# A fused recurrence and feed-forward kernel: copies shared with ScalarE, borrowed PSUM banks, a reordering store, unread matmuls and a fourth pair unit

One Trainium2 chip, one core. The metric is device time in microseconds (us) of one execution, median of several; lower is better.

## The reference

A gated linear recurrence for 4 batches of 8 heads, 768 steps, head size 48; its output is the input of a two-layer network with exact GELU.

```python
f = 1 / (1 + exp(-f_logit))
for t in range(768):
    state = f[:, :, t, :, None] * state + outer(k[:, :, t], v[:, :, t])
    y[:, :, t] = q[:, :, t] @ state
x = y.transpose(0, 2, 1, 3).reshape(3072, 384)
h = x @ w_in                       # 384 x 2048
g = 0.5 * h * (1 + erf(h / sqrt(2)))
return g @ w_out                   # 2048 x 384
```

## The kernel before

Sequences are cut into 24 chunks of 128 steps, two chunks to a unit, one feed-forward group for each unit. The kernel lists all operations with a guessed duration each. A greedy scheduler in the kernel's own Python sets the order of each engine, and also which buffer an operation gets. So the order on an engine is fixed before the run, and a wrong guess becomes a wait.

A "pair" unit puts steps 2p and 2p+1 next to each other, which lets its loads move 384-byte runs in place of 192. Then position j*64+p of a chunk's tile is step 2p+j, and something must put the steps back in order. Before, the copy of the transposed output did it:

```python
SIZES = [2] * 12
PAIRS = [0, 1, 2]
LOADS = ["u0", "u1", "i0", "i1", "i2", "i3", "u2", "o0", "o1", "o2", "o3"]   # then u3 ... u11
# ... (cut)
        def xcopy():                                     # xT: input of the first layer
            to = xT.t()[:, :, j * C:(j + 1) * C]
            if pair:
                nc.vector.tensor_copy(to.rearrange("a i (p s) -> a i s p", s=2),
                                      xpv().rearrange("a i (s p) -> a i s p", s=2))
            else:
                nc.vector.tensor_copy(to, xpv())
# ... (cut)
            P.add("DMA", 0.55, lambda n=n, osb=osb: nc.sync.dma_start(
                out=out[n * C:(n + 1) * C, :], in_=osb.t()), ...)      # the store of 128 rows
```

Loads of q, k, v and f_logit and all stores are issued by SP, in the order of its program. Weights are issued by GpSimd. TensorE's results go through eight PSUM banks: four for the feed-forward layers, two for attention's scores, two for the rest.

## Time and profile before

| | kernel before |
|---|---|
| median of 3 runs | 203.27 us (203.03 to 203.34) |
| profiled span | 200.9 us |
| TensorE / ScalarE / VectorE busy | 91% / 71% / 52% |
| DMA, mean over the span | 135 GB/s |

The lines that carry the reading of stages stand in the prediction. Loads and stores come through one queue; an issue takes 0.4 to 2.1 us between 40 and 64 us.

```profile
43.09 0.97 SPq L673 DMA_DIRECT2D out_dram<-osb  x2
44.11 0.45 SPq L351 DMA_DIRECT2D kt<-in_k_dram  x1
44.61 0.70 SPq L351 DMA_DIRECT2D qt<-in_q_dram  x1
45.35 1.00 SPq L351 DMA_DIRECT2D vt<-in_v_dram  x1
```

The first two stores are issued in 0.97 us and the next load follows at once. In the packets of the trace, the first store's 128 rows take 0.74 us from the first start to the last end.

### The profile page before, as it was taken

How to read it: one execution, taken by the hardware profiler on the slowest of the kernel's cores; microseconds unless marked ns; L12 is line 12 of the kernel's file. 1: busy time of each engine (PE TensorE's matmuls, PEld its weight loads, DVE VectorE, ACT ScalarE, POOL GpSimd, SP SyncE). 2: the span in 40 equal slices, each digit the busy share in tenths (PEclk: the TensorE clock that was granted, in tenths of full speed). 3: DMA queues.
4: the chain of work that ended last, by engine and by line, in shares of the span. 5: the costliest groups of instructions: out<-in, count | busy, mean ns of one | idle time of the engine just before them, and what ended most of it. 6: DMA issues, size and time to landing. Idle time of an engine off the chain costs nothing.

```text
span 200.9 us, 4982 instructions
## 1 busy us (share of the span) xinstructions
PE 182.2 (91%) x2010; PEld 141.7 (71%) x2010; DVE 103.7 (52%) x210; ACT 143.4 (71%) x243; POOL 52.4 (26%) x116
## 2 busy tenths in 40 slices
PE   0677989999989997997999999999999999999992
PEld 0446667687678687666868958967877969696961
DVE  4479661274386685887559728759778400000000
ACT  3642069989899979986999999769565828273740
POOL 7369236041133434105145411115303000000000
PEclk9999999999999999999999999999999999999999
DMA  6999999999899989989999993011001011110102
GB/s 155 261 224 172 175 269 189 182 220 202 181 216 195 182 203 186 203 177 210 182 197 214 191 214 96 3 39 39 3 0 65 16 42 39 38 44 11 68 0 78
DMA packets 93013, 27.04 MB, mean 135 GB/s; under 512 B 87872, under 2 KB 92480, under 8 KB 92992
## 3 DMA queue, kind: packets, MB, share of 16 engines
q1 hardware_dynamic: 90816, 23.60, 53.7%
q0 software_dynamic: 2176, 3.15, 9.4%
q8 instruction: 15, 0.25, 0.5%
q14 instruction: 6, 0.05, 0.1%
HBM read 25.17 MB, written 4.72 MB: 149 GB/s over the span
## 4 chain that ended last, share of the span: by engine, by line
PE 57%; ACT 20%; DMA 13%; SPq 3%; issue 3%; DVE 2%; POOL 1%; ACTq 0%; DVEq 0%
PE ps L667 25%; PE ps L652 20%; ACT L692 8%; ACT gT L657 6%; DMA fl<-in_f_logit_dram 5%; DMA win<-in_moe_w_in_dram 4%; DMA kt<-in_k_dram 3%; PE ps L444 3%; SPq L345 2%; ACT fl L368 2%; PE ps L535 2%; ACT lf L373 2%; PE ps L506 1%; ACT rg L400 1%; PE ps L385 1%
## 5 line engine op out<-in xcount | busy, mean ns | idle before, releaser
L652 PE MATMUL ps<-xT,win 128*128 128x256 bf16 x576 | 72.7, 277 | 3.1 <-ACT gT L657 3.0
L667 PE MATMUL ps<-wout,gT 128*128 128x384 bf16 x384 | 70.1, 326 | 0.4 <-DMA wout<-in_moe_w_out_dram 0.2
L652 PEld LDWEIGHTS <-win 128*128 128x128 bf16 x576 | 61.4, 115 | 6.0 <-issue 3.5
L657 ACT ACTIVATE gT<-ps 128x512 bf16<-128x512 f32 x96 | 53.1, 602 | 7.9 <-PE ps L652 5.6
L667 PEld LDWEIGHTS <-gT 128*128 128x128 bf16 x384 | 35.1, 97 | 21.3 <-ACT gT L657 1.3
L692 ACT ACT_TABLE_LOAD x29 | 37.2, 1283 | 0.5
L413 DVE TENSOR_TENSOR kp<-kt,rg 128x384 bf16<-128x384 f32 x24 | 13.9, 579 | 24.1 <-ACT rg L400 24.0
L671 ACT ACTIVATE osb<-ps 128x384 f32<-128x384 f32 x24 | 11.8, 493 | 20.2 <-PE ps L667 20.0
L456 DVE TENSOR_TENSOR am<-ps,mask 128x512 bf16<-128x512 f32 x36 | 23.1, 684 | 5.9 <-PE ps L535 5.8
L419 POOL CAST vb<-vt 128x384 bf16<-128x384 f32 x24 | 13.1, 554 | 43.7 <-DMA vt<-in_v_dram 43.4
L482 POOL TENSOR_TENSOR tn<-rr,gl 128x384 f32<-128x384 f32 x16 | 13.6, 850 | 41.5 <-DVE rr L480 38.7
L368 ACT ACTIVATE fl<-fl 128x768 f32<-128x768 f32 x12 | 10.3, 859 | 18.0 <-DMA fl<-in_f_logit_dram 17.9
L498 DVE CAST yb<-ps 128x384 bf16<-128x384 f32 x24 | 13.0, 553 | 11.9 <-PE ps L557 9.0
L449 DVE COPY kq<-ps 128x1024 bf16<-128x1024 bf16 x24 | 16.4, 685 | 3.3 <-PE ps L444 3.1
L487 POOL CAST sb<-tn 48x192 bf16<-48x192 f32 x40 | 15.3, 383 | 8.4 <-DVE tn L476 6.5
L400 ACT ACTIVATE rg<-ps 128x384 f32<-128x384 f32 x24 | 11.9, 495 | 6.8 <-PE ps L387 3.5
L416 DVE TENSOR_TENSOR qp<-qt,gt 128x384 bf16<-128x384 f32 x24 | 14.4, 601 | 0.2 <-ACT gt L402 0.2
L402 ACT ACTIVATE gt<-ps 128x384 f32<-128x384 f32 x24 | 11.9, 496 | 0.0
L444 PE MATMUL ps<-ident,kp 128*128 128x128 bf16 x96 | 10.2, 234 | 0.3 <-DVE kp L413 0.3
L456 DVE TENSOR_TENSOR am<-ps,maskp 128x512 bf16<-128x512 f32 x12 | 7.7, 685 | 5.4 <-PE ps L583 5.4
L444 PE MATMUL ps<-ident,qp 128*128 128x128 bf16 x96 | 10.2, 234 | 0.3 <-DVE qp L416 0.3
L373 ACT ACTIVATE lf<-fl 128x768 bf16<-128x768 f32 x12 | 10.1, 843 | 0.3
(58 smaller groups left out, 150.6 us busy)
## 6 DMA issues: line engine op xcount, KB each, us to landing
out_dram<-osb SPq DMA_DIRECT2D x24, 192.0 KB, 1.9
fl<-in_f_logit_dram SPq DMA_DIRECT2D x18, 192.0 KB, 3.8
kt<-in_k_dram SPq DMA_DIRECT2D x18, 192.0 KB, 3.7
qt<-in_q_dram SPq DMA_DIRECT2D x18, 192.0 KB, 3.8
vt<-in_v_dram SPq DMA_DIRECT2D x18, 192.0 KB, 3.7
win<-in_moe_w_in_dram POOLq DMA_DIRECT2D x4, 384.0 KB, 8.2
wout<-in_moe_w_out_dram POOLq DMA_DIRECT2D x4, 384.0 KB, 6.7
fl<-in_f_logit_dram SPq DMA_DIRECT2D x3, 384.0 KB, 4.2
```

The source lines that it names most:

```text
L368: P.add("ACT", 0.72, lambda: nc.scalar.activation(fl.t(), fl.t(), AF.Exp, scale=-1.0), rd=[("fl", n) for n in ns], wr=[("e", u)], bufs=[fl ...
L373: nc.scalar.activation(lf.t()[:, :, :, 0:D], v, AF.Ln, bias=1.0)
L400: P.add("ACT", 0.40, lambda g=gps[j], rg=rg: nc.scalar.activation(rg.t(), g.t()[:, 0:HD], AF.Exp, scale=-1.0), rd=[("g", n)], wr=[("rg", n ...
L416: P.add("DVE", 0.475, lambda y=y, gt=gt, j=j: nc.vector.tensor_tensor(y["qp"].t()[:, :, 0:D], half(u, x["qt"], j), gt.t().rearrange("p (h ...
L444: nc.tensor.transpose(tpv()[:, i, p, :], sr.t()[:, 2 * p:2 * p + 2, :], ident)
L449: P.add("DVE", 0.61, lambda tpv=tpv, kqv=kqv: nc.vector.tensor_copy(kqv(), tpv().rearrange("a i p (c t) -> a (i p) c t", c=2) if U[u]["pai ...
L456: P.add("DVE", 0.61, lambda hh=hh: nc.vector.tensor_tensor(ams[hh].t(), aps[hh].t().rearrange("p (h t) -> p h t", t=C), mk.unsqueeze(1).to ...
L487: P.add("POOL", 0.36, lambda hh=hh: nc.gpsimd.tensor_copy(sb.t()[64 * hh:64 * hh + D, :, D * hh:D * hh + D], tn.t()[64 * hh:64 * hh + D, : ...
L652: nc.tensor.matmul(hps.t()[:, i * tok:(i + 1) * tok], col(fo)[:, kk, :], xT.t()[:, kk, :], start=(kk == 0), stop=(kk == KO - 1))
L657: acts.append(P.add("ACT", 0.50, lambda u=u, hps=hps: nc.scalar.activation(gT.t()[:, u * pk:(u + 1) * pk, :].rearrange("p a b -> p (a b)") ...
L667: nc.tensor.matmul(op.t()[:, 0:d_model], gT.t()[:, fo, s_ * C:(s_ + 1) * C], wout[fo // 4][:, fo % 4, :], start=(fo == 0), stop=(fo == FO ...
L692: nc.scalar.preload_act_table_set({"exp": "natural_log_exp_and_others", "gelu": "gelu_and_others"}[o.table])
```

## The change

Its intent is a faster start (a warm TensorE, less on VectorE, no waits for the two attention banks), cheaper xT copies, fewer small load packets, and a scheduler with durations nearer to the trace. A warm TensorE is one at its full clock; unread matmuls, products of zeros whose result nobody reads, are to bring it there early.

```diff
-PAIRS = [0, 1, 2]
+PAIRS = [0, 1, 2, 3]
+EARLY = [0, 1]          # cumulative sums of these units use feed-forward banks
+HELP = [0, 1]           # ScalarE takes v casts, kq, yb and xT copies of these units
+WARM = 30.0             # unread matmuls in gaps that the plan shows before this time
@@ the store puts the steps in order, the copy no longer does
+    def rows(n):
+        r = out[n * C:(n + 1) * C, :]
+        return r.rearrange("(p j) m -> j p m", j=2) if U[n // 2]["pair"] else r
-            nc.vector.tensor_copy(to.rearrange(...), xpv().rearrange(...))    # pair units
+            copier(help_)(xT.t()[:, :, j * C:(j + 1) * C], xpv())
-                nc.sync.dma_start(out=out[n * C:(n + 1) * C, :], in_=osb.t())
+                nc.sync.dma_start(out=rows(n), in_=osb.t())
@@ unit 0's second score block
-            aps = [s_ap.new(), s_ap.new()]
+            aps = [(s_fh if jk and u == 0 else s_ap).new() for _ in range(2)]
@@ unread matmuls into the bank that the next real operation opens
+            if o.opens is not None and o.start < WARM:
+                for _ in range(int((o.start - at - 0.25) / (0.11 if o.start < 10 else 0.06))):
+                    nc.tensor.matmul(o.opens.t()[:, 0:C], junk, junk, start=True, stop=True, ...)
@@ durations in the plan: pair loads 1.2 -> 1.45, w_in 2.2 -> 2.56, w_out 2.2 -> 2.15,
@@ exponentials 0.72 -> 0.84, several matmul groups shorter; and a new rule for changing tables
```

More of the change, by code (lines that the diff above doesn't have):

```diff
@@ L59 @@
     __slots__ = ("eng", "dur", "fn", "bufs", "prio", "deps", "table", "start", "end", "vis", "seq", "name",
-                 "left", "outs", "inst", "chain")
+                 "left", "outs", "inst", "chain", "opens", "lag")
 class Plan:
@@ L68, in __init__, with add @@
         self.ops, self.w, self.r = [], {}, {}
-    def add(self, eng, dur, fn, rd=(), wr=(), bufs=(), prio=0.0, deps=(), table=None, name="", chain=None):
+    def add(self, eng, dur, fn, rd=(), wr=(), bufs=(), prio=0.0, deps=(), table=None, name="", chain=None, opens=None, lag=0.0):
         o = Op()
@@ L73, in add @@
         o.start = o.end = o.vis = o.inst = None
-        o.chain = chain
+        o.chain, o.opens, o.lag = chain, opens, lag
         o.seq = len(self.ops)
@@ L94, in run @@
         free["DMA"] = 1.8
-        act = None
+        act, switched = None, 0.0
         for o in self.ops:
@@ L108, in run @@
                 for d in o.deps:
-                    v = d.end if d.eng == o.eng and (o.eng != "DMA" or d is o.chain) else d.vis
+                    v = d.end if d.eng == o.eng and (o.eng != "DMA" or d is o.chain) else d.vis + o.lag
                     t = v if v > t else t
@@ L123, in run @@
                 if o.table and act and o.table != act:
-                    x = max(t, min(t + 2 * TABLE, max([d.vis for d in o.deps] + [0.0]) + PATIENCE))
+                    x = max(t, min(t + 2 * TABLE, max([d.vis for d in o.deps] + [switched]) + PATIENCE))
                 key = (int(x * 20 + 0.999), o.prio, o.seq)
@@ L132, in run @@
             if o.table and o.table != act:
-                act = o.table
+                act, switched = o.table, t
                 d += TABLE
@@ L158 @@
 SIZES = [2] * 12
-PAIRS = [0, 1, 2]
+PAIRS = [0, 1, 2, 3]
+EARLY = [0, 1]
+HELP = [0, 1]
+XDMA = []
+KDMA = []
+WARM = 30.0
 LOADS = ["u0", "u1", "i0", "i1", "i2", "i3", "u2", "o0", "o1", "o2", "o3"]
@@ L346 @@
                         out=x[nm].t().rearrange("p (h x) -> p h x", h=H), in_=srcp(a, m)),
-                        [(nm, 2 * m), (nm, 2 * m + 1)], [x[nm]], 1.2, f"{nm}{m}")
+                        [(nm, 2 * m), (nm, 2 * m + 1)], [x[nm]], 1.45, f"{nm}{m}")
             else:
@@ L355 @@
             load("pool", lambda m=m: nc.gpsimd.dma_start(out=win[m], in_=win_src[:, :, 512 * m:512 * m + 512]),
-                 [f"win{m}"], [], 2.2, what)
+                 [f"win{m}"], [], 2.56, what)
         else:
-            load("pool", lambda m=m: nc.gpsimd.dma_start(out=wout[m], in_=wo_src[m]), [f"wout{m}"], [], 2.2, what)
+            load("pool", lambda m=m: nc.gpsimd.dma_start(out=wout[m], in_=wo_src[m]), [f"wout{m}"], [], 2.15, what)
     def decays(u):
@@ L367, in decays @@
         flv = fl.t
-        P.add("ACT", 0.72, lambda: nc.scalar.activation(fl.t(), fl.t(), AF.Exp, scale=-1.0),
+        P.add("ACT", 0.84, lambda: nc.scalar.activation(fl.t(), fl.t(), AF.Exp, scale=-1.0),
               rd=[("fl", n) for n in ns], wr=[("e", u)], bufs=[fl], table="exp", prio=pr, name=f"E{u}")
@@ L373, in lnop @@
             nc.scalar.activation(lf.t()[:, :, :, 0:D], v, AF.Ln, bias=1.0)
-        P.add("ACT", 0.72, lnop, rd=[("e", u)] + z_lf, wr=[("lf", u)], bufs=[fl, lf], table="exp", prio=pr, name=f"L{u}")
-        gps = [s_m.new(), s_m.new()]
+        P.add("ACT", 0.84, lnop, rd=[("e", u)] + z_lf, wr=[("lf", u)], bufs=[fl, lf], table="exp", prio=pr, name=f"L{u}")
+        gps = [(s_fh if u in EARLY else s_m).new() for _ in range(2)]
         for j, n in enumerate(ns):
@@ L398, in decays @@
                   rd=[("lf", u)] + (["trip", "negp"] if pair else ["trin", "negcol"]), wr=[("g", n)],
-                  bufs=[lf, gps[j], gt, rg, y["kp"], y["qp"], gl], prio=pr, name=f"C{n}")
+                  bufs=[lf, gps[j], gt, rg, y["kp"], y["qp"], gl], prio=pr, opens=gps[j], name=f"C{n}")
             P.add("ACT", 0.40, lambda g=gps[j], rg=rg: nc.scalar.activation(rg.t(), g.t()[:, 0:HD], AF.Exp, scale=-1.0),
@@ L418, in decays @@
                 rd=[("gt", n), ("qt", n)] + z_qp, wr=[("qp", n)], bufs=[y["qp"], x["qt"], gt], prio=pr + 1, name=f"QP{n}")
-            P.add("POOL", 0.47, lambda y=y, j=j: nc.gpsimd.tensor_copy(
+            hv = u in HELP
+            P.add("ACT" if hv else "POOL", 0.40 if hv else 0.47, lambda y=y, j=j, hv=hv: (nc.scalar.copy if hv else nc.gpsimd.tensor_copy)(
                 y["vb"].t().rearrange("p (h d) -> p h d", h=H), half(u, x["vt"], j)),
@@ L423, with copier @@
     St = {}
+    def copier(act):
+        return nc.scalar.copy if act else nc.vector.tensor_copy
+    def rows(n):
+        r = out[n * C:(n + 1) * C, :]
+        return r.rearrange("(p j) m -> j p m", j=2) if U[n // 2]["pair"] else r
+    kqdeps = {n: [("kq", n)] for n in range(NCH)}
     def turn(u, kq):
@@ L430, in turn @@
             kp, qp = X[n]["kp"], X[n]["qp"]
+            if u in KDMA:
+                for i, (key, sr) in enumerate((("kp", kp), ("qp", qp))):
+                    P.add("DMA", 0.6, lambda i=i, sr=sr, j=j: nc.sync.dma_start_transpose(
+                        kq.t()[:, i, :, j, :], sr.t().rearrange("p h d -> p (h d)")),
+                        rd=[(key, n)], wr=[("tk" if i else "kq", n)], bufs=[sr, kq], prio=-6, lag=1.3, name=f"{key}D{n}")
+                kqdeps[n] = [("tk", n), ("kq", n)]
+                continue
             tp = s_m.new()
@@ L445, in turn @@
             P.add("PE", 0.225, lambda kp=kp, trans=trans: trans(0, kp), rd=[("kp", n), "ident"], wr=[("tk", n)],
-                  bufs=[tp, kp, kq], prio=pr + 4, name=f"Tk{n}")
+                  bufs=[tp, kp, kq], prio=pr + 4, opens=tp, name=f"Tk{n}")
             P.add("PE", 0.225, lambda qp=qp, trans=trans: trans(1, qp), rd=[("qp", n), "ident"], wr=[("tq", n)],
                   bufs=[tp, qp], prio=pr + 4, name=f"Tq{n}")
-            P.add("DVE", 0.61, lambda tpv=tpv, kqv=kqv: nc.vector.tensor_copy(
+            help_ = u in HELP and j == 0
+            P.add("ACT" if help_ else "DVE", 0.86 if help_ else 0.61, lambda tpv=tpv, kqv=kqv, help_=help_: copier(help_)(
                 kqv(), tpv().rearrange("a i p (c t) -> a (i p) c t", c=2) if U[u]["pair"]
@@ L467, in carry @@
             P.add("PE", mmdur, mm, rd=mmrd, wr=[("sp", n)], bufs=[sp, tn] + mmbufs + ([] if first_c else [rr]),
-                  prio=pr + 3.5, name=f"S{n}")
+                  prio=pr + 3.5, opens=sp, name=f"S{n}")
         def spf():
@@ L491, in carry, with outputs @@
         return sb
-    def outputs(n, yp, pair):
+    def outputs(n, yp):
         g, j = grp[n]
@@ L496, in outputs @@
         pr = 10 * n
-        yb, xp = X[n]["yb"], s_m.new()
-        P.add("DVE", 0.475, lambda: nc.vector.tensor_copy(yb.t(), yp.t()[:, 0:HD]),
+        yb = X[n]["yb"]
+        help_ = n // 2 in HELP and n % 2 == 1
+        P.add("ACT" if help_ else "DVE", 0.40 if help_ else 0.475, lambda: copier(help_)(yb.t(), yp.t()[:, 0:HD]),
               rd=[("yp", n)], wr=[("yb", n)], bufs=[yp, yb], prio=pr + 2, name=f"YB{n}")
+        if n // 2 in XDMA:
+            P.add("DMA", 0.5, lambda: nc.sync.dma_start_transpose(xT.t()[:, :, j * C:(j + 1) * C], yb.t()),
+                  rd=[("yb", n)], wr=[("x", n)], bufs=[yb, xT], prio=-7, lag=1.3, name=f"XD{n}")
+            return
+        xp = s_m.new()
         def xpv():
@@ L506, in xmm @@
                 nc.tensor.transpose(xpv()[:, i, :], yb.t()[:, i * C:(i + 1) * C], ident)
-        P.add("PE", 0.17, xmm, rd=[("yb", n), "ident"], wr=[("xp", n)], bufs=[yb, xp, xT], prio=pr + 1, name=f"XT{n}")
+        P.add("PE", 0.17, xmm, rd=[("yb", n), "ident"], wr=[("xp", n)], bufs=[yb, xp, xT], prio=pr + 1, opens=xp, name=f"XT{n}")
         def xcopy():
-            to = xT.t()[:, :, j * C:(j + 1) * C]
-            if pair:
-                nc.vector.tensor_copy(to.rearrange("a i (p s) -> a i s p", s=2), xpv().rearrange("a i (s p) -> a i s p", s=2))
-            else:
-                nc.vector.tensor_copy(to, xpv())
-        P.add("DVE", 0.27, xcopy, rd=[("xp", n)], wr=[("x", n)], bufs=[xp, xT], prio=pr + 1, name=f"X{n}")
+            copier(help_)(xT.t()[:, :, j * C:(j + 1) * C], xpv())
+        P.add("ACT" if help_ else "DVE", 0.39 if help_ else 0.27, xcopy, rd=[("xp", n)], wr=[("x", n)], bufs=[xp, xT], prio=pr + 1, name=f"X{n}")
     def inter(yp, lhs, osb, start):
@@ L536, in amm @@
                                          start=True, stop=True)
-            P.add("PE", 0.42, amm, rd=[("kq", n)], wr=[("ap", n)], bufs=[kq] + aps + ams, prio=pr + 3, name=f"A{n}")
+            P.add("PE", 0.36, amm, rd=kqdeps[n], wr=[("ap", n)], bufs=[kq] + aps + ams, prio=pr + 3, opens=aps[0], name=f"A{n}")
             mask_scores(aps, ams, ("am", n), f"AM{n}", ("ap", n), pr, mask, "mask")
@@ L559, in ymm @@
                                          skip_group_check=True)
-            P.add("PE", 0.36 + (0.175 if c else 0), ymm,
-                  rd=[("am", n, 0), ("am", n, 1), ("vb", n), ("kq", n)] + ([("sb", n - 1, 0), ("sb", n - 1, 1)] if c else []),
-                  wr=[("yp", n)], bufs=[yp, x["yb"], vb, kq] + ams + ([osb] if c else []), prio=pr + 2, name=f"Y{n}")
-            outputs(n, yp, False)
+            P.add("PE", 0.22 + (0.17 if c else 0), ymm,
+                  rd=[("am", n, 0), ("am", n, 1), ("vb", n)] + kqdeps[n] + ([("sb", n - 1, 0), ("sb", n - 1, 1)] if c else []),
+                  wr=[("yp", n)], bufs=[yp, x["yb"], vb, kq] + ams + ([osb] if c else []), prio=pr + 2, opens=yp, name=f"Y{n}")
+            outputs(n, yp)
     def attn_pair(u):
@@ L586, in attn_pair @@
             P.add("PE", 0.45, amm, rd=[("kq", n) for n in ns], wr=[("ap", u, jk)], bufs=[kq] + aps + ams[-1],
-                  prio=pr + 3, name=f"A{u}.{jk}")
+                  prio=pr + 3, opens=aps[0], name=f"A{u}.{jk}")
             mask_scores(aps, ams[-1], ("am", u, jk), f"AM{u}.{jk}", ("ap", u, jk), pr,
@@ L599, in attn_pair @@
         P.add("PE", 0.5, smm, rd=[("kp", n) for n in ns] + [("vb", n) for n in ns],
-              wr=[("sp", n) for n in ns[:len(sps)]], bufs=sps + kps + vbs, prio=pr + 3.5, name=f"S{u}")
+              wr=[("sp", n) for n in ns[:len(sps)]], bufs=sps + kps + vbs, prio=pr + 3.5, opens=sps[0], name=f"S{u}")
         osb = St.get("sb") if n0 % nC else None
@@ L622, in attn_pair @@
               wr=[("yi", n) for n in ns] + ([("yp", n0)] if osb is None else []), bufs=yps + vbs + sum(ams, []) + [X[n]["yb"] for n in ns],
-              prio=pr + 2, name=f"YI{u}")
+              prio=pr + 2, opens=yps[0], name=f"YI{u}")
         for cc, n in enumerate(ns):
@@ L627, in attn_pair @@
                 continue
-            P.add("PE", 0.26, lambda cc=cc, o=o: inter(yps[cc], lambda p: kq.t()[:, 1, p, cc, :], o, False),
+            P.add("PE", 0.18, lambda cc=cc, o=o: inter(yps[cc], lambda p: kq.t()[:, 1, p, cc, :], o, False),
                   rd=[("yi", n), ("sb", n - 1, 0), ("sb", n - 1, 1)] + [("kq", m) for m in ns], wr=[("yp", n)],
@@ L631, in attn_pair @@
         for cc, n in enumerate(ns):
-            outputs(n, yps[cc], True)
+            outputs(n, yps[cc])
     def ffn_group(g, gate):
@@ L655, in ffn_group @@
                   rd=[("x", n) for n in ns] + [f"win{i}" for i in sorted({(u * pk + i) // 4 for i in range(pk)})],
-                  wr=[("h", g, u)], bufs=[xT, hps, gT], prio=pr, name=f"F1.{g}.{u}")
+                  wr=[("h", g, u)], bufs=[xT, hps, gT], prio=pr, opens=hps, name=f"F1.{g}.{u}")
             acts.append(P.add("ACT", 0.50, lambda u=u, hps=hps: nc.scalar.activation(
@@ L672, in ffn_group @@
                   rd=[("o", n)], wr=[("os", n)], bufs=[op, osb], prio=pr - 1000, name=f"O{n}")
-            P.add("DMA", 0.55, lambda n=n, osb=osb: nc.sync.dma_start(out=out[n * C:(n + 1) * C, :], in_=osb.t()),
+            P.add("DMA", 0.55, lambda n=n, osb=osb: nc.sync.dma_start(out=rows(n), in_=osb.t()),
                   rd=[("os", n)], bufs=[osb], prio=-5, name=f"st{n}")
@@ L687 @@
     state = {}
+    junk = one.tile([C, C], BF16, name="junk")
+    nc.gpsimd.memset(junk, 0.0)
+    at = 0.9
     for o in P.placed:
+        if o.eng == "PE":
+            if o.opens is not None and o.start < WARM:
+                for _ in range(int((o.start - at - 0.25) / (0.11 if o.start < 10 else 0.06))):
+                    nc.tensor.matmul(o.opens.t()[:, 0:C], junk, junk, start=True, stop=True, skip_group_check=True)
+            at = o.end
         if o.table and state.get("t") != o.table:
```

## The prediction

> **What bounds the kernel now.** I read the page first, then busy time by stretch, then ScalarE's and TensorE's timelines of the start, the waits, and the chain that ended last. The page's slices, each 5.02 us, for TensorE, ScalarE and DMA:
>
> ```profile
> PE   0677989999989997997999999999999999999992
> ...
> ACT  3642069989899979986999999769565828273740
> ...
> DMA  6999999999899989989999993011001011110102
> ```
>
> The reader is to see three stages: a start with TensorE and ScalarE poorly used, a middle (to about 120 us) with TensorE, ScalarE and DMA all near nine tenths, and an end in which TensorE alone is full. Busy time by stretch (PE, PEld, DVE, ACT and POOL busy us with instruction counts, then clock, DMA share and GB/s):
>
> ```profile
> 6.00:22.00 16.00, 12.41 (x168) 8.98 (x169) 12.61 (x23) 5.54 (x13) 8.89 (x15) 1.00 1.20 214
> 22.00:30.00 8.00, 7.21 (x101) 5.13 (x98) 4.85 (x9) 2.95 (x4) 2.73 (x6) 1.00 1.08 229
> 30.00:40.00 10.00, 9.71 (x79) 7.24 (x78) 1.65 (x4) 9.91 (x16) 3.46 (x7) 1.00 1.00 186
> 40.00:120.00 80.00, 75.99 (x913) 59.13 (x912) 52.46 (x99) 73.74 (x121) 24.41 (x48) 1.00 0.96 198
> 120.00:160.00 40.00, 39.62 (x484) 32.34 (x483) 29.92 (x56) 29.14 (x56) 8.12 (x15) 1.00 0.11 36
> 160.00:201.00 41.00, 37.29 (x280) 28.76 (x277) 0.00 (x0) 19.45 (x34) 0.00 (x0) 1.00 0.11 39
> ```
>
> A busy PE is not yet a fast PE, so I made a ledger from start times: late in the trace a first-layer matmul (128x256) starts every 109 ns and a second-layer one (128x384) every 163 ns. 576 x 0.109 + 384 x 0.163 = 125 us; the chain of waits agrees (48 first-layer in 5.24 us, 32 second-layer in 5.20 us, so 10.44 us for each of 12 groups). Attention's matmuls, each at its own full-speed spacing, add 40.4 us. Total work 165.6 us of a 200.9 us span, so 35.3 us are lost: 6.4 before the first matmul, 13.1 up to 30 us (10.5 us of work done there), 12.0 from 30 to 160 us (8.7 of them between 40 and 120), 3.8 in the tail. From 120 us on almost nothing is lost, so **what the change gains must be TensorE work done earlier, mostly before 40 us.**
>
> Why the start is poor, TensorE (start, duration, line):
>
> ```profile
> 22.56 2.75 PE L652 MATMUL ps<-xT,win 128*128 128x256 bf16 x12
> ...
> 25.81 1.93 PE L652 MATMUL ps<-xT,win 128*128 128x256 bf16 x12
> ...
> 29.83 0.82 PE L652 MATMUL ps<-xT,win 128*128 128x256 bf16 x6 [0.31 <-ACT gT L657]
> ...
> 30.65 2.78 PE L652 MATMUL ps<-xT,win 128*128 128x256 bf16 x24
> ```
>
> Twelve matmuls take 2.75 us at 22.56, and twenty-four take 2.78 us at 30.65. Single starts are 213 ns apart up to 26.7 us and 109 ns after it. The page's clock column shows 1.00 in both, so that column does not show this halving; the spacing does. Next ScalarE:
>
> ```profile
> 27.02 0.85 ACT L368 ACTIVATE fl<-fl 128x768 f32<-128x768 f32 x1 [10.53 <-DMA fl<-in_f_logit_dram]
> 27.89 1.28 ACT L692 ACT_TABLE_LOAD   x1
> 29.18 3.04 ACT L657 ACTIVATE gT<-ps 128x512 bf16<-128x512 f32 x6
> 32.24 1.28 ACT L692 ACT_TABLE_LOAD   x1
> 33.54 0.84 ACT L373 ACTIVATE lf<-fl 128x768 bf16<-128x768 f32 x1
> ```
>
> ScalarE stands idle 10.53 us for the third unit's f_logit, although the first layer's results have been there since about 24 us. Its order put the third unit's exponential ahead of the first GELU. Four banks fill by 27.7 us and TensorE waits until a GELU frees one, at 29.8.
>
> **What the Trainium skill says.** "TensorE: Matmul & The Clock Gate", Part 1: the array runs at half rate until one window of about 3.4 us has been busy, and goes back after an idle window. The trace agrees in size (213 against 109 ns); here scattered work from 6.4 us did not lift it before 26.7. The same page says queues of ScalarE and VectorE are strict FIFO: the 10.53 us wait in front of ready GELUs is that. "ScalarE: Activation LUTs", What ACT_TABLE_LOAD costs: about 1283 ns a load plus a drain of about 1380; the trace has 1283 ns, but the GELU starts 1.29 us after the load began, so I use 1.28. No run here shows the extra drain.
>
> **The change, part by part**, from the order of instructions on each engine.
>
> *Unread matmuls.* 99 of 128x128 in eight gaps: 44 ahead of the first real one, then 5, 12, 9, 9, 4, 5, and 11. At the half-rate spacing seen for 128x128 transposes, 107 ns, the 44 take 4.7 us, from about 1.2 to 5.9 us, beside the wait for f_logit, which lands at about 4.6 us whatever TensorE does. If that lifts the clock by about 7 us, attention's matmuls of two units cost about half (6.7 instead of 11 to 13 us), some of it hidden behind VectorE. The groups write to a bank that must be free, and stand ahead of real work: the 11 can push the second group's first layer back by 11 x 0.056 = 0.6 us at worst.
>
> *ScalarE help in units 0 and 1.* It takes 4 casts of v (off GpSimd, 0.51 each), 2 kq copies (VectorE 0.69 each; about 1.0 on ScalarE), 2 yb copies (0.56 against 0.49) and 2 xT copies (0.59 against 0.49). VectorE, busy 12.61 of 16 us here, loses 2 x (0.69 + 0.56 + 0.59) = 3.7 us. ScalarE gains about 6 us in stretches where it idles, except that the first v cast waits in its queue for a landing at about 9.1 us and holds a kq copy behind it to about 9.6.
>
> *Feed-forward banks.* The cumulative sums of units 0 and 1, and the second score block of unit 0, no longer wait for the two attention banks: about 1 us (12.7 to 13.3 and the 0.81 us VectorE wait ahead of its masks).
>
> Walking the chain with these durations: kq of unit 0 complete at 10.5 instead of 11.1, decayed keys of unit 1 from 14.7 instead of 15.5; but the carry copies still wait behind GpSimd's four weight issues, to 15.66. So the cross term at 16.6, yb 17.6, xT 18.2 to 19.1, and the first layer at **about 19.3 instead of 22.56**. The first weight quarter lands at 18.0, the others at 21.0, 22.8 and 24.7, so the rest of the first group is paced by data and ends about 27.6.
>
> *Order on ScalarE.* All eight GELUs of group 0 now stand before the third unit's exponential. They run from about 20.4 to 28.5 us; then load, exponential, logarithm, load, five GELUs, load, and the decay exponentials of unit 2 at about 37.1 instead of 38.58. At the same point of attention 13 GELUs are done instead of 9: 4 x 0.51 + 1.5 = **3.5 us ahead**. TensorE's ledger at 40 us: attention of two units 6.7, first layer 15 x 0.656 = 9.8, second layer of group 0 5.2, unit 2 about 1.0: 22.7 against 19.6 before, **3.1 us ahead**. The second layer cannot start before its weights land at about 33.6, as before.
>
> *Fourth pair unit.* Its loads become 4 issues with 384-byte packets in place of 8 with 192-byte ones. Unit 3 loaded from 37.3 to 48.4 us in halves; a pair at the 260 GB/s of units 0 and 1 takes 1.57 MB / 260 = 6 us, so later loads may be about 4 us sooner. It costs TensorE about 0.65 us (four 162 ns sums instead of two, 16 carry matmuls of 43 ns instead of 8).
>
> *Reordered store.* xT copies for pairs fall from 588 to 348 ns (6 x 0.24 on VectorE); the store keeps 1536-byte rows, so no cost.
>
> *New order in the middle.* 31 table loads instead of 29, +2.6 us on ScalarE; against that, two f_logit waits of 3.2 us together after 40 us should shrink, as loads come sooner and the plan's durations for them are longer, nearer to the trace. I count 2.2 of the 8.7 us lost there as won.
>
> Sum on the span: -3.1 (start) -2.2 (middle) +0.65 = -4.6; 203.3 - 4.6 = 198.7, rounded to **198.8**.
>
> **Rivals.** (1) *ScalarE takes over as the bound* from 40 to 120 us: 73.7 of 80 us is busy and two loads more are due, so a lead of 3 us shrinks to about 1; then 201 to 202. For it: chains of load, GELU, load in the chain that ended last. Against: fewer waits there and four GELUs less to do. (2) *The start is bound by transfers* and the warm clock is hidden: weights land when they landed, DMA share is full from 2 us. If only the GELU order counts, -2 us: 201. Against: four banks were full and TensorE waited at 28 to 30 us. (3) *Larger gain*: the sooner loads let the middle run with half its losses, 195 to 196. (4) *Unread matmuls or ScalarE's queue delay real work*: a cast that waits for v holds everything behind it; 1 us, still not slower than before.
>
> **Range and chances.** The start's gain has several supports (2 to 4 us). The middle is a whole new order with everything near nine tenths, and can give 4 us or take 2. So 195 to 202 us. Two per cent is 199.2 us, just above my estimate: faster 0.56, same 0.42, slower 0.02.
>
> **What would show it.** Right: spacing of first-layer matmuls 109 ns from their first, which starts near 19.3 us; first GELU near 20.4; no wait of 10 us for f_logit; TensorE's work at 40 us about 22.7 us; all loads landed by about 118 instead of 122. Wrong: 213 ns spacing past 20 us, first-layer starts waiting for weights, more than 9 us lost between 40 and 120 us, or ScalarE over 95% there.

## The result

The changed kernel took **222.34 us** (220.71 to 222.68, 4 fast runs) against 203.31 us for the kernel before: ratio 1.0914, 95% interval 1.0851 to 1.0976. It is slower by 9%, far outside the range. A ratio here is the mean time of one kernel's fast runs over that of the other's in the same rounds, so not quite the ratio of the medians.

The page of the changed kernel (40 slices of 5.52 us; PEclk is the granted clock in tenths):

```profile
PE   7769998994838999785994299999999999999993
...
ACT  4767699773038969488962798999964764746551
...
PEclk9996999999695999999998569999999999999999
DMA  7999899635466983788379996930101002010101
```

In the kernel before, the DMA row showed 8 and 9 up to 120 us. Here it drops to 3, 5, 4 and 6 from 44 us on, and the holes in TensorE's and ScalarE's rows come with it. The start is as intended, in TensorE's timeline:

```profile
1.00 4.13 PE L724 MATMUL ps<-junk 128*128 128x128 bf16 x44 [1.00 <-POOL junk L718]
6.19 0.32 PE L397 MATMUL ps<-lf,trip 128*128 128x384 bf16 x1 [1.06 <-ACT lf L380]
...
20.00 2.09 PE L681 MATMUL ps<-xT,win 128*128 128x256 bf16 x12
```

The first layer starts at 20.0 us (22.56 before), and the first GELU at 21.5 us (29.18 before). The ledger of TensorE's work, made as in the prediction and without the unread matmuls:

| work done by TensorE, us, up to | 22 us | 40 us | 60 us | 80 us | 120 us |
|---|---|---|---|---|---|
| before | 6.1 | 19.6 | 37.4 | 54.9 | 90.8 |
| changed | 6.9 | 22.3 | 35.8 | 48.5 | 79.4 |

At 40 us the changed kernel is 2.7 us ahead. The loss begins after that. SP's timeline there:

```profile
43.10 1.31 SPq L702 DMA_DIRECT2D out_dram<-osb  x2
44.47 0.52 SPq L352 DMA_DIRECT2D qt<-in_q_dram  x1
45.05 5.65 SPq L352 DMA_DIRECT2D vt<-in_v_dram  x1
50.74 2.93 SPq L358 DMA_DIRECT2D fl<-in_f_logit_dram  x1
```

and the chain that ended last (start, duration, what):

```profile
44.47 10.51 DMA qt<-in_q_dram
...
80.92 10.20 DMA vt<-in_v_dram
```

Both long transfers of the chain were issued right behind stores of pair units (the first behind two in a row, the second behind two with one load between them). SP is held by the issue of v for 5.65 us. Busy time between 43 and 57 us, first the kernel before, then the changed one (last two columns: DMA share, GB/s):

```profile
43.00:57.00 14.00, 13.98 (x178) 10.61 (x177) 7.05 (x14) 12.36 (x21) 2.25 (x6) 1.00 0.91 199
```

```profile
43.00:57.00 14.00, 9.99 (x138) 6.76 (x137) 6.08 (x12) 6.71 (x13) 0.67 (x2) 0.94 0.39 104
```

The core moves half as many bytes and its DMA engines are mostly idle, while loads wait. The packets of the trace tell why. "In flight" is the summed time of a store's packets over the time from its first to its last:

| first store of a pair unit | first to last packet | packets in flight |
|---|---|---|
| before | 0.74 us | 11.7 |
| changed | 5.05 us | 2.1 |

The eight stores of pair units took 3.9 to 5.3 us each; the sixteen stores of other units, later in the same run, took 0.7 at the median. The page's own view of issues does not show it: its median from issue to landing of a store is 1.9 us in both kernels, and asked for 40 to 60 us alone it gives no landing for the stores of the changed kernel at all.

The Trainium skill has the rule, which I had not looked up for the store: "DMA: Bandwidth & Descriptors", section Why a DMA increments its semaphore by 16 and not by 1, says that a transfer runs on the largest number of engines, up to 16, that divides the size of the slowest dimension (of those larger than 1) on both sides. The reordered output is 2 x 64 x 384, so that number is 2. The trace agrees: 2.1 packets in flight. It shows the split in the loads too. The load of q issued at 44.47 us has 1024 packets of 384 bytes. Of these 896, fourteen sixteenths, run from 45.7 to 47.6 us, beside the first store. The next load, v, does the same from 51.4 to 53.4 us. The 128 packets that each of the two still lacks start only when the second store has ended, at 53.4 us.

### The profile page after: what moved, and what is told of

Its sections match the earlier page's. It is cut to its first block, busy times and chain, and to the rows that moved or that the text cites.

```text
span 220.9 us, 5252 instructions
## 1 busy us (share of the span) xinstructions
PE 189.7 (86%) x2151; PEld 148.9 (67%) x2151; DVE 101.1 (46%) x204; ACT 151.6 (69%) x254; POOL 48.9 (22%) x113
## 4 chain that ended last, share of the span: by engine, by line
PE 54%; DMA 21%; SPq 8%; ACT 6%; issue 4%; POOL 4%; DVE 2%; POOLq 0%; ACTq 0%; DVEq 0%
PE ps L681 22%; PE ps L696 21%; DMA vt<-in_v_dram 10%; SPq L358 5%; DMA qt<-in_q_dram 5%; DMA fl<-in_f_logit_dram 3%; DMA kt<-in_k_dram 3%; PE ps L469 3%; ACT L729 2%; SPq L352 2%; PE ps L564 2%; POOL win L362 1%; PE ps L548 1%; ACT gT L686 1%; PE ps L539 1%
## 5 line engine op out<-in xcount | busy, mean ns | idle before, releaser
L681 PE MATMUL ps<-xT,win 128*128 128x256 bf16 x576 | 75.7, 284 | 11.6 <-ACT gT L686 11.5
L681 PEld LDWEIGHTS <-win 128*128 128x128 bf16 x576 | 62.4, 116 | 15.7 <-issue 11.8
L375 ACT ACTIVATE fl<-fl 128x768 f32<-128x768 f32 x12 | 10.2, 847 | 25.8 <-DMA fl<-in_f_logit_dram 25.8
L427 POOL CAST vb<-vt 128x384 bf16<-128x384 f32 x20 | 10.3, 518 | 68.3 <-DMA vt<-in_v_dram 68.0
L525 DVE CAST yb<-ps 128x384 bf16<-128x384 f32 x22 | 12.0, 555 | 22.9 <-PE ps L586 13.2
L482 DVE TENSOR_TENSOR am<-ps,mask 128x512 bf16<-128x512 f32 x32 | 20.6, 684 | 4.1 <-PE ps L564 4.1
L420 DVE TENSOR_TENSOR kp<-kt,rg 128x384 bf16<-128x384 f32 x24 | 13.4, 560 | 19.6 <-ACT rg L407 17.4
L423 DVE TENSOR_TENSOR qp<-qt,gt 128x384 bf16<-128x384 f32 x24 | 14.5, 605 | 10.2 <-ACT gt L409 5.4
L475 DVE COPY kq<-ps 128x1024 bf16<-128x1024 bf16 x22 | 15.1, 688 | 6.6 <-PE ps L469 5.7
L543 DVE COPY xT<-ps 128x384 bf16<-128x384 bf16 x22 | 7.8, 354 | 14.1 <-PE ps L539 14.0
L482 DVE TENSOR_TENSOR am<-ps,maskp 128x512 bf16<-128x512 f32 x16 | 10.2, 685 | 6.0 <-PE ps L612 6.0
L539 PE MATMUL ps<-ident,yb 128*128 128x128 bf16 x72 | 8.3, 230 | 4.3 <-DVE xT L543 4.0
```

Source lines behind the costliest of these rows:

```text
L420: P.add("DVE", 0.475, lambda y=y, rg=rg, j=j: nc.vector.tensor_tensor(y["kp"].t()[:, :, 0:D], half(u, x["kt"], j), rg.t().rearrange("p (h ...
L423: P.add("DVE", 0.475, lambda y=y, gt=gt, j=j: nc.vector.tensor_tensor(y["qp"].t()[:, :, 0:D], half(u, x["qt"], j), gt.t().rearrange("p (h ...
L475: P.add("ACT" if help_ else "DVE", 0.86 if help_ else 0.61, lambda tpv=tpv, kqv=kqv, help_=help_: copier(help_)(kqv(), tpv().rearrange("a ...
L482: P.add("DVE", 0.61, lambda hh=hh: nc.vector.tensor_tensor(ams[hh].t(), aps[hh].t().rearrange("p (h t) -> p h t", t=C), mk.unsqueeze(1).to ...
L525: P.add("ACT" if help_ else "DVE", 0.40 if help_ else 0.475, lambda: copier(help_)(yb.t(), yp.t()[:, 0:HD]), rd=[("yp", n)], wr=[("yb", n) ...
L681: nc.tensor.matmul(hps.t()[:, i * tok:(i + 1) * tok], col(fo)[:, kk, :], xT.t()[:, kk, :], start=(kk == 0), stop=(kk == KO - 1))
```

## The experiments

All ratios are to the kernel before in the same rounds. Medians and ratios are of fast runs; where some runs were slow, the number of fast ones is given.

| run | median us, fast runs | ratio | 95% interval |
|---|---|---|---|
| changed kernel | 222.34 | 1.0914 | 1.0851 to 1.0976 |
| e1_undo_store | 198.70 | 0.9791 | 0.9730 to 0.9851 |
| e1_again (same kernel) | 200.11 (4 of 6) | 0.9827 | 0.9772 to 0.9882 |
| e2_split_store | 202.63 | 0.9981 | 0.9907 to 1.0055 |
| e3_store_alone | 219.40 | 1.0793 | 1.0712 to 1.0874 |
| e4_sixteen (wrong) | 198.26 | 0.9772 | 0.9714 to 0.9831 |
| e9_four (wrong) | 211.64 | 1.0418 | 1.0373 to 1.0463 |
| e12_split_plain | 204.12 (13 of 20) | 1.0008 | 0.9979 to 1.0037 |
| e15_other_queue | 220.70 | 1.0786 | 1.0715 to 1.0857 |
| e16_plain_other_queue | 199.76 | 0.9798 | 0.9760 to 0.9836 |
| e5_no_unread | 200.23 | 0.9843 | 0.9789 to 0.9898 |
| e6_no_help_no_banks | 199.07 | 0.9763 | 0.9712 to 0.9814 |
| e7_three_pairs | 200.94 (10 of 20) | 0.9860 | 0.9831 to 0.9890 |
| e10_plan_alone | 202.92 (16 of 20) | 0.9950 | 0.9923 to 0.9978 |
| e8_gap_filled | 199.15 | 0.9790 | 0.9747 to 0.9833 |

The kernel before had medians of 202.6, 203.6, 203.4 and 203.8 us in the four calls, so medians of different calls are not compared to better than half a per cent.

### Is it the store?

Three theories: the store is slow (A); the new order puts stores that wait for ScalarE ahead of loads (B); the falling clock costs the time (C).

**e1_undo_store.** The order on every engine stays; the copy reorders again.

```diff
-        return r.rearrange("(p j) m -> j p m", j=2) if U[n // 2]["pair"] else r
+        return r
-            copier(help_)(xT.t()[:, :, j * C:(j + 1) * C], xpv())
+            (pair units: the copy with "(p s) -> s p", as before)
```

> The changed kernel with the pair positions put right by the xT copy again, as before, and plain stores; every engine keeps its order. Theory A (the reordered store itself is slow: its 128 rows took 5.0 us from first to last packet at 44.4 to 49.4 us, against 0.7 us for a store of the kernel before, and the loads behind it in the queue wait): the eight stores go back to about 0.7 us, loads land by about 120 us and the time is 196 to 201 us. Rival B (the new order puts two stores ahead of unit 3's q and v loads in the SP queue, where they wait for ScalarE until 43.1 us, and the loads come late whatever the store costs): 212 us or more. Rival C (the clock fell to half four times because TensorE's work is too scattered, and that costs the 20 us): 215 or more.

Measured 198.70 us, ratio 0.9791. Theory A stands. B falls: SP's order is that of the changed kernel, and its store still waits for ScalarE until 41.64 us. C falls as a first cause: in the profiled run, the page's clock row shows nothing below 8. SP's timeline:

```profile
41.64 1.01 SPq L706 DMA_DIRECT2D out_dram<-osb  x2
42.70 0.45 SPq L352 DMA_DIRECT2D qt<-in_q_dram  x1
43.20 0.67 SPq L352 DMA_DIRECT2D vt<-in_v_dram  x1
43.92 1.63 SPq L358 DMA_DIRECT2D fl<-in_f_logit_dram  x1
```

The v issue that took 5.65 us takes 0.67. Busy time of this run in the same stretch:

```profile
43.00:57.00 14.00, 13.28 (x204) 9.58 (x202) 10.12 (x19) 8.93 (x14) 3.05 (x6) 1.00 0.96 217
```

**e3_store_alone.** The other direction: the kernel before with nothing but the reordered store and the plain copy.

```diff
-            P.add("DMA", ..., nc.sync.dma_start(out=out[n * C:(n + 1) * C, :], in_=osb.t()))
+            P.add("DMA", ..., nc.sync.dma_start(out=rows(n), in_=osb.t()))
```

> The kernel before with the reordered store alone (three pair units, so six such stores; the xT copy in plain order). Theory A: six stores of about 5 us on two engines hold up the loads behind them by up to 4 us each while DMA is the fullest engine: 211 to 225 us. Rivals B and C: 203, perhaps 1 us less, as six xT copies fall from 588 to 348 ns.

Measured 219.40 us, ratio 1.0793. Its six stores of pair units took 4.0 to 5.0 us. The store alone makes most of the loss, as theory A expected.

### Is it the number of engines, or the scattered rows?

**e4_sixteen** and **e9_four** deal the rows out by 16 and by 4. Their results are wrong (relative error 0.81 in both); the number of rows and bytes is the same, and rows lie further apart than with 2.

```diff
-        return r.rearrange("(p j) m -> j p m", j=2) if ...
+        return r.rearrange("(p j) m -> j p m", j=16) if ...     # e9_four: j=4
```

> The changed kernel with the store's rows dealt out by 16 instead of by 2 (row 16p+j from position j): a wrong result on purpose in the pair units. Rows are further apart than in the changed kernel, but the output side's slowest dimension is 16. Theory A in the narrower form: a store takes about 0.7 us again and the time is that of the split store, 196 to 201 us. If scattered rows are what is slow: 222 us or more.

> The changed kernel with the store's rows dealt out by 4 (row 4p+j from position j; a wrong result on purpose in the pair units). If the transfer is spread over as many engines as the output side's slowest dimension: a store takes about 2.5 us (5.0 with 2, about 0.8 with 16), and the time lies between, 201 to 210 us. If 2 is special and any other form is fast: 198 to 199 us.

| slowest dimension of the output | first store, first to last packet | packets in flight | mean of the eight stores | ratio |
|---|---|---|---|---|
| 2 (changed) | 5.05 us | 2.1 | 4.59 us | 1.0914 |
| 4 (e9_four) | 3.63 us | 3.5 | 3.26 us | 1.0418 |
| 16 (e4_sixteen) | 0.86 us | 13.5 | 1.42 us | 0.9772 |

Packets in flight follow the dimension, and rows far apart cost nothing that the time shows. With 4 a store took longer than the 2.5 us that I expected, and the time of 211.64 us lies just above the 201 to 210.

**e2_split_store** gives the right result with two stores of 64 rows, one for each position in the pair.

```diff
-  nc.sync.dma_start(out=rows(n), in_=osb.t())
+  [nc.sync.dma_start(out=v, in_=osb.t()[s, :]) for v, s in halves(n)]   # rows j, j+2, ... from partitions 64j to 64j+63
```

> The changed kernel, but each reordered store is issued as two stores of 64 rows, one for each position in the pair, so that the slowest dimension of the output side is 64 and not 2. Theory A in its narrower form (the transfer is spread over as many engines as the slowest dimension of the output side allows, 2): each half takes about 0.4 us, the time is 196 to 201 us, within 1 us of the run with the store undone. If instead rows that are not next to each other are slow: about 222 us as the changed kernel. Rivals B and C: 212 or more.

Measured 202.63 us, ratio 0.9981. The stores are wide again (1.24 us, 10.5 in flight), but 4 us of the gain are missing. The expectation of 196 to 201 us missed.

**e12_split_plain** asks why: plain rows in order, also in two halves.

> The changed kernel with the store undone, but the plain stores of pair units issued as two stores of 64 rows. The split reordered store took 202.6 us, 4 us more than a single plain store; this tells why. If it is the second issue in the SP queue (about 0.6 us each, 8 of them, ahead of loads): 201 to 203 us here too. If it is the scattered rows: 198 to 199.5 us.

Measured 204.12 us, a little above what the second issue was expected to cost; ratio 1.0008 against 0.9827 for the whole plain store in the same rounds. So rows out of order are not the reason; splitting is. In e2_split_store two stores, four issues, held SP for 2.46 us ahead of the loads, where e1_undo_store needed 1.01 us. Part of the difference can be the clock, which fell to half twice in the profiled runs of e2_split_store and e12_split_plain. What share each has is open.

### How does a slow store reach the loads?

**e15_other_queue** keeps the slow store and issues it from ScalarE's queue; **e16_plain_other_queue** does the same to a plain store.

```diff
-  nc.sync.dma_start(out=rows(n), in_=osb.t())
+  (nc.scalar if U[n // 2]["pair"] else nc.sync).dma_start(out=rows(n), in_=osb.t())
```

> The changed kernel with its eight reordered stores, still on two engines, issued from ScalarE's queue and not from SP's; loads stay in SP's. If the damage is that loads stand behind the slow store in the same queue: each store still takes 4 to 5 us and about 2 packets are in flight, but the loads pass it: 199 to 206 us. If the damage is the two busy engines themselves, which every load also needs: 214 us or more.

> The changed kernel with the store undone (plain, 16 engines), with the pair units' stores in ScalarE's queue. It gives what the move itself does to a store that is not slow. SP no longer waits for ScalarE's results ahead of loads (its waits there were about 30 us before 120 us), against some 0.5 us of ScalarE for each issue: 196 to 199 us; if the issues cost ScalarE more than SP's waits cost the loads: 199 to 201.

e15 took 220.70 us, ratio 1.0786: next to no rescue. e16 took 199.76 us, ratio 0.9798, so the move by itself is harmless. In e15 the eight stores took 4.7 to 5.7 us each, with 1.7 to 1.9 packets in flight. In e15, SP's load issues are held although no store is in its queue:

```profile
47.09 0.65 SPq L358 DMA_DIRECT2D vt<-in_v_dram  x1
47.79 5.21 SPq L358 DMA_DIRECT2D fl<-in_f_logit_dram  x1
53.04 4.55 SPq L358 DMA_DIRECT2D kt<-in_k_dram  x1
```

The same skill page, in Issuing engines are not separate DMA queues, says that transfers issued by different engines share the same 16 DMA engines. The packets of e15 fit that. From 51.0 to 53.5 us the trace has 68 packets of a store and 68 of a load: 1.8 and 0.4 in flight, and next to nothing else, although the load's other packets are done. So the two take turns on the two engines, and the load is not done until its share there is. In the changed kernel, with one queue, the load's share waited behind both stores; in e15 it runs between the store's packets, and the time is hardly better. I had favoured the queue; the run speaks for the engines. Why SP's next issue is held meanwhile, with the other engines idle, no run shows. ScalarE was held by its first issue of two stores for 4.67 us in e15, but for 4.08 us in e16 too, so that is not what separates the two by 21 us.

### What the other parts are worth

All on the base of e1_undo_store.

**e5_no_unread**, `WARM = 0`: same order, no unread matmuls.

> The changed kernel with the store undone (198.7 us) and now without the 99 unread matmuls; all else keeps its order. Theory A (they lift TensorE's clock from about 4 us on and bring the first layer forward): half-rate spacing (213 ns) returns up to some point between 17 and 27 us, the first layer starts 0.5 to 1.5 us later, and the time is 199.7 to 201.5 us. Rival B (transfers and ScalarE set the start, a warm array is hidden): 198.5 to 199.2.

200.23 us, ratio 0.9843. The first layer starts at 19.7 us instead of 19.0, at a half-rate spacing of 0.19 us on the mean of its first eleven steps. At 40 us TensorE has done 22.3 us of work instead of 23.5. But this half rate need not come from the missing matmuls: the clock fell at 18.1 us, as it did at 17.8 us in the changed kernel, which has them and starts its first layer at 213 ns too. The median is in theory A's range. The intervals of the ratios overlap (0.9791 and 0.9827 with the matmuls), so a gain of 0.2 to 0.5% is possible and not shown.

**e6_no_help_no_banks**, `HELP = []`, `EARLY = []`, scores of unit 0 in their own banks.

> The same base without ScalarE's copies in units 0 and 1 and without the feed-forward banks for attention; the scheduler makes a new order. Theory A (the early chain is worth about 1.5 to 2 us): 200 to 201.5 us. Rival B (only the place of the GELUs ahead of the third unit's exponential counts, and that comes from the corrected durations): 198.5 to 199.5.

199.07 us, ratio 0.9763: nothing is lost. The first layer starts at 23.1 us instead of 19.0, and at 40 us TensorE is 2.8 us behind e1_undo_store (20.7 against 23.5), yet the end is the same. Between 40 and 120 us it then does 73.4 us of work against 72.8. Rival B's size was right, its reason was not: e10_plan_alone below also has the first GELUs (from 23.6 us) ahead of the third unit's exponential (32.8 us; its profiled run is a slow one, but the order is the plan's), and gains only half a per cent.

**e7_three_pairs**, `PAIRS = [0, 1, 2]`.

> The same base with three pair units, as before the change. Theory A (the fourth pair brings later loads forward by up to 4 us, and loads pace the middle): 200 to 202 us. Rival B (it costs TensorE 0.65 us and hides its gain behind TensorE's backlog): 197.5 to 198.7.

200.94 us, ratio 0.9860. Its interval overlaps with those of e1_undo_store and e1_again, and its profiled run was slow, so no line of it is read. The fourth pair may be worth half a per cent; this is open.

**e10_plan_alone** has the new durations and table rule alone.

> The kernel before with only the scheduler's corrected durations and its new rule for changing tables: no unread matmuls, no ScalarE help, no borrowed banks, three pairs, store and xT copy as before. If the corrected order is the main part of the gain: 199.5 to 201. If the parts that shorten the early chain carry it: 202 to 204.

202.92 us, ratio 0.9950. The corrected plan is worth about half a per cent. e5, e6 and e7 each lie clearly below it in the same rounds, so no single one of the other parts carries the rest. e6 differs from e10 by the unread matmuls and the fourth pair, with the new order that they bring: 0.9763 against 0.9950. How these share the 1.9% is open.

**e8_gap_filled** adds 22 unread matmuls where TensorE idled and the clock had fallen in some runs.

```diff
-  for _ in range(int((o.start - at - 0.25) / ...)):
+  for _ in range(int((o.start - at - 0.25) / ...) + (22 if o.name == "Tk2" else 0)):
```

> The changed kernel with the store undone, and 22 more unread matmuls (about 1.2 us) ahead of the first transposes of unit 1, where TensorE stood idle 1.3 us and the clock fell back in some runs (17.8 to 21.3 us in the changed kernel's trace). If that fall costs time: no half clock between 4 and 190 us and 0.5 to 1 us less than the same kernel without the 22 in the same rounds (197.5 to 198.3). If not: the same within 0.3 us. A candidate to beat both kernels.

199.15 us, ratio 0.9790, against 0.9827 for **e1_again** in the same rounds:

> The changed kernel with the store undone once more, as the neighbour of the other runs here: ratio to the kernel before 0.973 to 0.985 as the first time.

e1_again came out as expected; e8 missed its 197.5 to 198.3 us. Its profiled run has a full clock from 5.9 to 197 us, but the difference of the two ratios is inside their intervals. Both beat the kernel before and the changed one, and so does e6_no_help_no_banks.

## Why the prediction was wrong

The step that failed is one sentence of the prediction: "the store keeps 1536-byte rows, so no cost". I looked at the size of a row and not at how a transfer is divided among engines. In its place the runs showed stores of 4.6 us on two engines. Putting the store back takes the ratio from 1.0914 to 0.9791 and takes some 23 us off; adding the store alone to the kernel before costs 7.9%. No rival of mine contained it either: the rival about transfers spoke of loads alone.

The other steps, read from e1_undo_store where the store does not hide them:

| step | predicted | measured |
|---|---|---|
| first layer starts | 19.3 us | 19.0 us (20.0 in the changed kernel) |
| first GELU | 20.4 us | 20.2 us (21.5) |
| TensorE's work at 40 us | 22.7 us | 23.5 us (22.3) |
| lost between 40 and 120 us | 6.5 us of 8.7 before | 7.2 us (22.9) |
| last load lands | about 118 us | 121.2 us (146.2) |
| cost of the fourth pair on TensorE | 0.65 us | 0.8 us (total work 166.3 against 165.5) |
| time | 198.8 us | 198.70 and 200.11 us (222.34) |

So the sum without the store was about right, in part by luck. I took the early lead of TensorE as the gain, and e6_no_help_no_banks, with 2.8 us less of it, ends as early. The 2.2 us to be won in the middle are not shown either: in the profiled run of e1_again, the same kernel as e1_undo_store, TensorE's work at 40 us is 22.8 us, but about 10 us are lost between 40 and 120 us, more than the 8.7 before, with one fall of the clock (3.4 us at 105.5 us). And the prediction's own sum of 198.7 was rounded the wrong way, to 198.8.

The reading of the clock stands as far as the trace shows it. With the 44 unread matmuls the clock records start at full rate at 4.2 us (6.7 in e1_undo_store, 14.7 without them in e5_no_unread, 26.8 in the kernel before). In the changed kernel they fall to half for 3.4 us at 17.8 us, and again for 3.4, 6.8 and 10.2 us after 55 us: TensorE starves for loads then, and e1_undo_store has no such fall before 194 us, so the later ones probably follow from the stall. They may add to it: those later 20.5 us at half rate are within the 9%, and I did not separate them.

## What to carry to other kernels

When a change alters only the access pattern of a transfer, check the slowest dimension on both sides first: a reordered output of 2 x 64 rows ran on two engines and cost more than all else gained. Here a slow transfer held up the loads that shared its engines, whichever queue it came from; look for it in the DMA share falling while loads wait, and in packets in flight, not in the median time to landing. And before a bundle of changes is judged, undo its parts one at a time: here one line hid a gain of about 2% (0.9791 and 0.9827).

## What the Trainium skill lacked or had wrong

- "DMA: Bandwidth & Descriptors", Why a DMA increments its semaphore by 16 and not by 1: the rule for the number of engines held (2.1, 3.5 and 13.5 packets in flight for 2, 4 and 16). It gives no figure for what a transfer on few engines does to others: with 8 stores of 192 KB each on two engines the ratio was 1.0914, against 0.9791 with the stores undone; issued from another queue, 1.0786 against 0.9798.
- The same page advises against two transfers to disjoint partition halves (Rules for kernel authors), but gives no price for a store split in two. Here: 1.0008 against 0.9827 for the whole store, in the same rounds.
- "TensorE: Matmul & The Clock Gate", Part 1: it does not say whether matmuls on zeros count as activity. Here, with 44 of them, 4.13 us long, the clock records start at full rate at 4.2 and 6.7 us, and without them at 14.7 us. Its window of about 3.4 us agrees: half-rate stretches lasted 3.4, 6.8 and 10.2 us.
- "ScalarE: Activation LUTs", What ACT_TABLE_LOAD costs: the drain of about 1380 ns that comes on top of each load is not seen here; a load of 1.28 us begins 0.02 us after the end of the activation before it (27.02 + 0.85 us, then 27.89), and the next activation starts 1.29 us after the load began.
